# Talking-heads attention and SoLU block: ten source rows in one transfer, pairs in column halves, 64x64 score tiles, and a planner with measured durations

## The chip, the cores and the metric

The kernel runs on one core of a Trainium2 chip. The metric is the device time of one execution in microseconds. An execution has five engines with instruction streams of their own, which run in the order in which they were written and wait for each other by semaphores: TensorE (PE), VectorE (DVE), ScalarE (ACT), GpSimd (POOL), and SyncE (SP), which only issues transfers here. The transfers themselves are made by 16 DMA engines.

## The reference

```python
# q, k, v: (4, 12, 448, 64) = batch, heads, positions, head size
scores = scale * np.matmul(q, k.transpose(0, 1, 3, 2))
scores = np.einsum('bhij,hg->bgij', scores, w_pre)      # mix the heads
scores = scores - np.max(scores, axis=-1, keepdims=True)
attn = np.exp(scores)
attn = attn / (np.sum(attn, axis=-1, keepdims=True) + 1e-09)
attn = np.einsum('bhij,hg->bgij', attn, w_post)         # mix them again
out = np.matmul(attn, v)
# then x = out as (1792, 768)
h = x @ w_in                                            # (768, 1024)
e = np.exp(h - max(h)); sm = e / (sum(e) + 1e-09)
solu = h * sm
ln = (solu - mean(solu)) / np.sqrt(var(solu) + 1e-06) * g_ln
return ln @ w_out                                       # (1024, 768)
```

## The kernel before

For the scores, the first mixing and the second part, numbers of 32 bits are split into a high and a low part of 16 bits, and a product is made of three matmuls (high by low, low by high, high by high). The second mixing and the value products take 32 bits as they are.

A batch has 448 query rows. They are cut into four blocks, of 120 rows or of 88 (`ROWS`, `SIZES`), and a block into units of ten rows (`UN`), 12 units or 9, so that a batch has 45 units and the kernel 180. A unit holds ten query rows for all 12 heads, that is 120 partitions of 448 keys.

- **Scores.** `qk` makes the scores of two heads for a whole block: six matmuls, each 64 rows of the array by the block's 120 or 88 columns, the two heads beside each other in the two row halves. `score_hi` (ACT) and `score_lo` (DVE) write them as high and low parts into the tile `s`, which has a query row on each partition and 12 heads, two parts and 448 keys behind it.
- **Fetch.** The mixing over heads needs the 12 heads on partitions. `fetch` turns each unit by transfers from SBUF to SBUF: five source rows (five partitions of `s`) become 60 partitions of the tile `sr`, one per row and head. A unit takes two such transfers, for its two halves, which lie side by side in `sr`; the two units of a pair lie on partitions 0 to 59 and 64 to 123. All are issued by SP, at line 524. `sr` has four buffers (`AHEAD`), one for each pair, and is free again when the units' row maxima have been taken, since these write their unused full-size output over it.
- **Premix.** `premix` (line 540) mixes the heads for both units of a pair, in twelve matmuls in 64x64 tiles: PSUM tile `pm`, three banks (`m`).
- **Softmax.** `rowmax` (DVE, line 552), `expo` (ACT, line 565, with the sum of the exponentials), `guard` (DVE, line 579, adds 1e-9), `invert` (DVE, line 582), and `weigh` (POOL, line 586), which multiplies the second mixing matrix by the inverse sums into `wr`. There is one of each for every unit.
- **Postmix and values.** `postmix` (line 594) multiplies the exponentials by `wr`; `post_out` (ACT) copies the result into the ring `p_t`; once a block is complete, `av` (line 634) multiplies it by the values, in two bursts of 24 matmuls; `x_hi` and `x_lo` split the result and `x_store` (line 676) writes it out.

Beside this run the loads and the splitting of the next batch's q, k and v; 18 transposing transfers for q and k (`turn_in`, line 427, issued by SP too); and in the last batch the loads and the conversion of `w_in`. After the attention comes the second part, with 14 tiles of 128 tokens.

The order of the whole attention part is written out by a planner, the class `Plan`. Each step is a task with engines and costs, tasks that it follows (`after`), a due time, and the ring of buffers that it holds until other tasks are done. `order` simulates the engines, always places the task that can start earliest, and among those that can start within 0.005 us of it the one due first. A transfer's cost in it is the issue time on SP and a constant latency (`lat`):

```python
                add(
                    ("f",) + g,
                    one(fetch, *g),
                    {"sp": 1.3},
                    after=[("sl", b, blk, h) for h in range(H)],
                    ...
                    until=[("mx",) + p for p in pair],
                    lat=2.7,
                )
```

The tasks' names: `qk`, `sh` and `sl` for the scores, `f` for the fetch, `m` for the premix, `mx`, `ex`, `gd`, `iv`, `w` for the softmax, `o` and `po` for the postmix and its copy, `av`, `xh`, `xl`, `xd` for what follows, `t` for the transposing transfers.

Of the kernel before, what the change touches and what calls it, by code (L numbers as in the profile page):

```python
# [8 lines left out]
F32 = mybir.dt.float32  # L9
# [9 lines left out]
class Plan:  # L19
# [4 lines left out]
    WAIT = 0.2  # L24
    SWITCH = {("m", "o"): 0.087, ("av", "o"): 0.073, ("m", "av"): 0.057, ("o", "qk"): 0.04, ("o", "m"): 0.026}
# [5 lines left out]
    def add(self, key, run, on, after=(), behind=(), due=0.0, ring=None, until=(), lat=0.0, more=()):  # L31

        slots = [list(until)] + [list(x) for x in more]
        self.tasks[key] = (run, on, list(after), due, ring, slots, lat, list(behind))

    def order(self):
        tasks, done, out = self.tasks, {}, []
        held = {r: [] for r in self.size}
        free = {e: 0.0 for _, on, *_ in tasks.values() for e in on}
# [5 lines left out]
        avail = {k for k, n in need.items() if not n}  # L45

        def ready(k, e):
            _, _, after, _, ring, slots, _, _ = tasks[k]
            r = 0.0
            for a in after:  # L50
                end, eng, lat = done[a]
                r = max(r, end + lat + (0.06 if eng == e else self.WAIT))
            for i in range(len(slots) if ring else 0):
                j = len(held[ring]) + i - self.size[ring]
                for a in held[ring][j] if j >= 0 else ():
                    if a not in done:
                        return None
                    r = max(r, done[a][0] + done[a][2] + self.WAIT)
            return r

        last = {}
        while len(out) < len(tasks):
            best = None
            for e, t0 in free.items():
                able = []
                for k in avail:
                    on = tasks[k][1]
                    if e in on:
                        r = ready(k, e)
                        if r is not None:  # L70
                            able.append((max(r, t0), tasks[k][3], k))
                while able:
                    t = min(x[0] for x in able)
                    x = min(
                        (x for x in able if x[0] <= t + 0.005),
                        key=lambda x: (x[1] + 40 * self.SWITCH.get((last.get(e), x[2][0]), 0), str(x[2])),
                    )
                    on = tasks[x[2]][1]
                    if any(max(ready(x[2], f), free[f]) + c < t + on[e] for f, c in on.items() if f != e):
                        able.remove(x)  # L80
                        continue
                    if best is None or (t, x[1]) < best[:2]:
                        best = (t, x[1], e, x[2])
                    break
            t, _, e, k = best
            run, on, _, _, ring, slots, lat, _ = tasks[k]
            free[e] = t + on[e] + 0 * self.SWITCH.get((last.get(e), k[0]), 0)
            last[e] = k[0]
            done[k] = (t + on[e], e, lat)
# [12 lines left out]
def kernel(  # L102
# [30 lines left out]
    WEIGH = {"pool": 0.36}  # L133
    AMV = {"act": 0.95}
# [131 lines left out]
    def chain(key, steps, due, after=()):  # L266

        for i, (eng, f) in enumerate(steps):
# [3 lines left out]
                {eng: 0.3 if eng == "pe" else 0.15},  # L272
# [10 lines left out]
    mk = const.tile([128, 2, UH], F32, name="mk")  # L283
    mh = const.tile([128, UH], F32, name="mh")
# [8 lines left out]
    def mix_load(e):  # L293
        nc.gpsimd.memset(rep, 0.0)
        for i, w in ((0, w_pre), (1, w_post)):
            for lo in (0, 64):
                nc.gpsimd.dma_start(out=rep[lo : lo + HK, i], in_=w.unsqueeze(0).to_broadcast([UH, H, H]))

    def mix_masks(e):
        nc.gpsimd.memset(mk, 1.0)  # L300
        for step, base in ((1, 0), (-1, H - 1)):
            nc.gpsimd.affine_select(
                out=mk,
                in_=mk,
                pattern=[[-64 * step, 2], [-H * step, UH]],
                compare_op=ALU.is_ge,
                fill=0.0,
                base=base,
                channel_multiplier=step,
            )  # L310
        nc.gpsimd.tensor_tensor(out=mh, in0=mk[:, 0], in1=mk[:, 1], op=ALU.add)
# [156 lines left out]
    def qk(b, c, h):  # L468
# [6 lines left out]
        for a, (x, y) in enumerate(((0, 1), (1, 0), (0, 0))):  # L475
            for e in range(2):
                rows = slice(64 * e, 64 * e + 64)
                nc.tensor.matmul(  # L478
                    sps[b, c, h + e],
                    q2[b, g][rows, 2 * j + x, i0 : i0 + n],  # L480
                    k1[b, g][rows, 2 * j + y],
                    start=(a == 0),
                    stop=(a == 2),
                )
# [30 lines left out]

    def fetch(b, u):
        c, r, step, _ = unit_rows(b, u)
        u0, _ = pair_of(b, u)
        if u == u0:
            sr[b, u] = sr_p.tile([128, 2, 2, S], F16, tag="sr", name=f"sr_{b}_{u}")  # L520
        lo = 64 * (u - u0)
        for i in range(2):
            r0 = r + i * UH * step
            nc.sync.dma_start(  # L524
                out=sr[b, u0][lo : lo + HK, i], in_=s_t[b, c][r0 : r0 + (UH - 1) * step + 1 : step]
            )

    def premix(b, u):
# [4 lines left out]
        x = sr[b, u]  # L533
        for j in range(n):
            pmx[b, u + j] = ps_m.tile([UK, 512], F32, tag="m", name=f"pm_{b}_{u + j}")
        for a, (w, z) in enumerate(((wp_hi, 0), (wp_hi, 1), (wp_lo, 0))):
            for j in range(n):
                rows = slice(64 * j, 64 * j + HK)
                for i in range(2):
                    nc.tensor.matmul(  # L540
                        pmx[b, u + j][64 * i : 64 * i + 64, 0:S],
                        w[rows],
                        x[rows, i, z],
# [4 lines left out]
    def rowmax(b, u):  # L548
        nb = nbs[b, u] = st_p.tile([UK, 1], F32, tag="nb", name=f"nb_{b}_{u}")
        u0, _ = pair_of(b, u)  # L550
# [11 lines left out]
    def expo(b, u):  # L562
        sm = sums[b, u] = st_p.tile([UK, 1], F32, tag="sm", name=f"sm_{b}_{u}")
# [10 lines left out]
    def guard(b, u, eng):  # L574
        sm = sums[b, u]
        if eng == "pool":
            nc.gpsimd.tensor_scalar(out=sm, in0=sm, scalar1=1e-9, scalar2=1.0, op0=ALU.add, op1=ALU.mult)
        else:
            nc.vector.tensor_scalar(out=sm, in0=sm, scalar1=1e-9, scalar2=None, op0=ALU.add)

    def invert(b, u):
        nc.vector.reciprocal(out=sums[b, u], in_=sums[b, u])  # L582

    def weigh(b, u, eng):
        w = wr[b, u] = st_p.tile([UK, H * UN], F32, tag="wr", bufs=NWR, name=f"wr_{b}_{u}")
        ENG[eng].tensor_scalar(  # L586
            out=w, in0=wq[0:UK, 0 : H * UN], scalar1=sums.pop((b, u)), scalar2=1.0, op0=ALU.mult, op1=ALU.mult
# [18 lines left out]
    def post_out(b, u, eng):  # L606
        i, n = ring_of(b, u), unit_rows(b, u)[3]
        y = pos.pop((b, u))[:, 0:480].rearrange("p (c i) -> p c i", i=UN)
        copy(eng, p_t[:, :, i : i + n], y[:, :, UN - n : UN])
# [17 lines left out]
    def av(b, blk, g):  # L627
        n = block_rows(b, blk)[1]
        xps[b, blk, g] = ps_x.tile([128, XG, 512 // XG], F32, tag="x", name=f"px_{b}_{blk}_{g}")
        for i in range(XG):  # L630
# [175 lines left out]
    def add_tasks():  # L806
# [5 lines left out]
        add("mixl", mix_load, {"pool": 4.2}, due=0.0, lat=7.5)  # L812
        add("mixm", mix_masks, {"pool": 1.2}, due=1.0)
# [17 lines left out]
        for b in range(B):  # L831
# [3 lines left out]
            for n in "kq":  # L835
                pieces = NP if z else NPAIR
                parts = [(f, n, b, p) for p in range(NPAIR) for f in ("hi", "lo")]
                for i in range(pieces):
# [3 lines left out]
                        {"pool": 1.06} if b else {"sp": 0.65},  # L842
# [5 lines left out]
                        lat=2.6 if b else 4.0 + 0.7 * i + 5.0 * (n == "q"),  # L848
# [4 lines left out]
                for i in range(NP):  # L853
# [3 lines left out]
                        {"dve": 0.93},  # L857
# [8 lines left out]
                for p in range(NPAIR):  # L866
# [4 lines left out]
                        {"pool": 0.8} if b else {"act": 0.61},  # L871
                        after=ready + ([("hi", n, b, p - 1)] if p else before),
# [559 lines left out]
```

## Time and profile before

| | |
|---|---|
| time, median of 3 runs | 804.56 us (802.21 to 805.5) |
| the profiled execution | 801.89 us, of it 800.2 us span |
| PE busy | 684.1 us, 85% of the span |
| DVE busy | 503.2 us, 63% |
| ACT busy | 454.1 us, 57% |
| POOL busy | 264.2 us, 33% |
| mean granted TensorE clock | 0.935 |

The span runs from the first instruction to the last. Busy times are of one profiled execution, and matmuls are pipelined, so that a busy PE is not one at its peak. SP's own instructions, which issue the transfers, are not counted as busy. The clock is a share of full speed, 2.4 GHz; it has two levels, 1.0 and 0.5. The kernel has roughly three stages: the start up to 40 us, the attention up to 550 us, and the second part to the end.

### The profile page before, as it was taken

The numbers are of one execution on the slowest core, as the hardware profiler recorded it, in microseconds if no ns is written. First come the engines' busy times: TensorE is split into PE (matmuls) and PEld (weight loads), VectorE is DVE, ScalarE is ACT, GpSimd is POOL, SyncE is SP. The second block draws the span as 40 slices with busy tenths as digits, with TensorE's granted clock in tenths as the row PEclk, the third lists the DMA queues.
The fourth block names the chain that finished last, engine by engine and source line by source line (L and its number), as shares of the span: only waits on it lengthen the run. The fifth ranks groups of instructions, "written<-read, shape, count | busy, mean of one in ns | idle before, by whom it ended". The sixth has DMA issues, their size and how long they took to land.

```text
span 800.2 us, 16611 instructions
## 1 busy us (share of the span) xinstructions
PE 684.1 (85%) x5986; PEld 443.2 (55%) x5986; DVE 503.2 (63%) x1519; ACT 454.1 (57%) x962; POOL 264.2 (33%) x408
## 2 busy tenths in 40 slices
PE   4878895998987798779699597979998776999998
PEld 3435563765755566557376474757443333556664
DVE  6947883678795578777376798865888866220000
ACT  3746675776676687568477576745455555331111
POOL 5224671124580122563011234232365552330000
PEclk9879998999999799799699799979999997999999
DMA  8044487236458434648614564632646630434111
GB/s 207 13 130 140 143 152 155 106 117 197 158 141 143 124 107 136 189 138 151 145 67 144 177 199 145 166 111 94 178 106 129 134 67 1 90 55 106 57 43 59
DMA packets 114057, 98.45 MB, mean 123 GB/s; under 512 B 69636, under 2 KB 104632, under 8 KB 113976
## 3 DMA queue, kind: packets, MB, share of 16 engines
q1 hardware_dynamic: 108120, 83.62, 40.4%
q0 software_dynamic: 4448, 12.40, 5.6%
q10 hardware_dynamic: 1408, 1.38, 0.7%
q8 instruction: 47, 0.77, 0.4%
q14 instruction: 34, 0.28, 0.1%
HBM read 33.24 MB, written 9.63 MB: 54 GB/s over the span
## 4 chain that ended last, share of the span: by engine, by line
PE 41%; DMA 21%; DVE 15%; SPq 9%; issue 5%; ACT 5%; POOL 4%; DVEq 0%; ACTq 0%; POOLq 0%
PE y L1341 13%; DMA sr<-s 12%; PE po L594 9%; PE px L634 7%; SPq L524 7%; PE ps L478 4%; PE pm L540 4%; DMA cv_wo<-in_moe_w_out_dram 3%; DMA raw_k<-in_k_dram 3%; PE ps_h L797 3%; DVE sr L552 2%; DVE s L495 2%; DMA xl<-xsl 2%; SPq L427 1%; ACT e L565 1%
## 5 line engine op out<-in xcount | busy, mean ns | idle before, releaser
L594 PE MATMUL po<-wr,e 128*112 128x120 f32 x1440 | 196.0, 286 | 14.8 <-POOL wr L586 14.3
L594 PEld LDWEIGHTS po<-wr,e 128*112 128x112 f32 x1440 | 169.0, 187 | 64.7 <-POOL wr L586 32.1
L586 POOL TENSOR_SCALAR wr<-wq,sm 128x120 f32<-128x120 f32 x180 | 72.1, 402 | 335.6 <-DVE sm L582 196.9
L565 ACT ACTIVATE e<-pm,nb,c_exp 128x448 f32<-128x448 f32 x180 | 131.2, 730 | 46.5 <-DVE sr L552 33.2
L552 DVE TENSOR_SCALAR_CACHE_REDUCE sr<-pm,c_nexp 128x448 f32<-128x448 f32 x180 | 118.8, 675 | 54.8 <-PE pm L540 54.1
L230 ACT COPY p_t<-po 112x480 f32<-112x480 f32 x180 | 104.3, 581 | 54.7 <-PE po L594 53.9
L495 DVE SCALAR_TENSOR_TENSOR s<-ps,s 120x448 f16<-120x448 f32 (+1 forms) x192 | 114.5, 616 | 31.1 <-ACT s L490 29.6
L490 ACT ACTIVATE s<-ps 120x448 f16<-120x448 f32 (+1 forms) x192 | 99.5, 544 | 52.1 <-PE ps L478 37.7
L540 PE MATMUL pm<-sr,wp_hi 60*64 60x448 f16 x720 | 78.5, 384 | 49.0 <-DMA sr<-s 35.6
L478 PE MATMUL ps<-k,q 64*120 64x448 f16 (+1 forms) x576 | 84.9, 388 | 10.8 <-DVE s L495 9.9
L797 PE MATMUL ps_h<-wi,xf 128*128 128x512 f16 x396 | 87.9, 379 | 6.7 <-DVE u L1284 6.7
L634 PE MATMUL px<-p_t,raw_v 112*64 112x120 f32 (+1 forms) x1536 | 83.8, 267 | 2.0 <-DVE xsl L226 1.6
L634 PEld LDWEIGHTS px<-p_t,raw_v 112*64 112x64 f32 x1536 | 77.0, 141 | 9.5 <-ACT p_t L230 4.2
L1341 PE MATMUL y<-wo_h,lth 128*128 128x384 f16 (+2 forms) x224 | 72.7, 331 | 9.8 <-ACT wo_h L221 9.8
L1341 PE MATMUL y<-wo_l,lth 128*128 128x384 f16 (+2 forms) x224 | 73.0, 333 | 2.5 <-DVE wo_l L226 2.0
L1341 PE MATMUL y<-wo_h,ltl 128*128 128x384 f16 (+2 forms) x224 | 72.9, 332 | 0.0
L1341 PEld LDWEIGHTS <-lth 128*128 128x128 f16 x448 | 44.3, 99 | 43.8 <-issue 15.4
L797 PEld LDWEIGHTS <-xf 128*128 128x128 f16 x396 | 38.4, 98 | 52.5 <-issue 8.6
L540 PEld LDWEIGHTS <-wp_hi 60*64 60x64 f16 x720 | 19.6, 106 | 83.1 <-issue 45.6
L1349 ACT ACTIVATE o<-y,c_out 128x384 f32<-128x384 f32 (+2 forms) x28 | 16.1, 577 | 70.7 <-PE y L1341 70.7
L478 PEld LDWEIGHTS <-q 64*120 64x120 f16 (+1 forms) x576 | 33.5, 133 | 40.5 <-issue 30.2
L226 DVE SCALAR_TENSOR_TENSOR xsl<-px,x_sc,xsh 128x120 f16<-128x120 f32 (+1 forms) x104 | 27.0, 317 | 28.0 <-ACT xsh L221 21.6
(175 smaller groups left out, 845.4 us busy)
## 6 DMA issues: line engine op xcount, KB each, us to landing
sr<-s SPq DMA_DIRECT2D x360, 105.0 KB
cv_wi<-in_moe_w_in_dram SPq DMA_DIRECT2D x24, 256.0 KB
cv_wo<-in_moe_w_out_dram SPq DMA_DIRECT2D x8, 768.0 KB
raw_k<-in_k_dram POOLq DMA_DIRECT2D x18, 224.0 KB, 6.3
raw_q<-in_q_dram POOLq DMA_DIRECT2D x18, 224.0 KB, 6.0
raw_v<-in_v_dram POOLq DMA_DIRECT2D x18, 224.0 KB, 6.2
xh<-xsh SPq DMA_DIRECT2D x9, 224.0 KB
xl<-xsl SPq DMA_DIRECT2D x9, 224.0 KB
```

The source lines that it names most:

```text
L230: nc.scalar.copy(out=out, in_=in_)
L478: nc.tensor.matmul(sps[b, c, h + e], q2[b, g][rows, 2 * j + x, i0 : i0 + n], k1[b, g][rows, 2 * j + y], start=(a == 0), stop=(a == 2),)
L490: nc.scalar.activation(out=s_t[b, c][0 : y.shape[0], h, 0], in_=y, func=AF.Copy, scale=2.0**-E_S)
L495: nc.vector.scalar_tensor_tensor(out=t[:, h, 1], in0=y, scalar=2.0**-E_S, in1=t[:, h, 0], op0=ALU.mult, op1=ALU.subtract)
L540: nc.tensor.matmul(pmx[b, u + j][64 * i : 64 * i + 64, 0:S], w[rows], x[rows, i, z], start=(a == 0), stop=(a == 2),)
L552: nc.vector.tensor_scalar(out=old, in0=pmx[b, u][:, 0:S], scalar1=c_nexp[0:UK, b : b + 1], scalar2=None, op0=ALU.mult, op1=ALU.min, accum_ ...
L565: nc.scalar.activation(out=ee[b, u], in_=pmx.pop((b, u))[:, 0:S], func=AF.Exp, bias=nbs.pop((b, u)), scale=c_exp[0:UK, b : b + 1], accum_o ...
L586: ENG[eng].tensor_scalar(out=w, in0=wq[0:UK, 0 : H * UN], scalar1=sums.pop((b, u)), scalar2=1.0, op0=ALU.mult, op1=ALU.mult)
L594: nc.tensor.matmul(ps[:, c * 120 : (c + 1) * 120], e[:, c * CP : (c + 1) * CP], w, start=True, stop=True)
L634: nc.tensor.matmul(xps[b, blk, g][e * 64 : e * 64 + 64, i, 0:n], raws["v", b][:, h, c * D : (c + 1) * D], block_view(b, blk, c * H + h), s ...
L797: nc.tensor.matmul(ps[:, n], xx[:, kc, o : o + 128], ww[:, kc, n * 512 : (n + 1) * 512], start=(kc == 0 and a == 0), stop=(kc == KDM - 1 a ...
L1341: nc.tensor.matmul(y, xx[:, kc], ww[:, kc, cut], start=(kc == 0 and a == 0), stop=(kc == KFF - 1 and a == 2),)
```

## The change

`fetch` issues one transfer for each unit of a pair: all ten source rows, onto the partitions 4 to 123 of `sr`. The two units of a pair now lie in the two column halves of the tile, and the two halves of a unit's rows below each other. A premix output so holds one half of the rows of both units, and `post_out` writes it to the ring with an access pattern of two runs. A block's odd last unit still takes two transfers of five rows. The four tiles of `sr` are allocated once, and their first four partitions set to zero by DVE at the start. `rowmax` writes its unused output to a tile `dead` of its own, so that `sr` is free after the premix. `guard` and `invert` are done once for a pair, after both exponentials. `qk` makes the scores of a 120-row block in twelve matmuls of 64x64 tiles (56 columns in half of them). `av` is a task for each of six pairs of heads, of 8 matmuls, in place of two tasks of 24.

The planner's model is another one: each task has an occupancy and a time to its result; hearing of a result costs a time by engine; PE pays 0.093 us when the tile shape changes; a transfer is put on 16 modelled rings with a latency, a size and a rate; the task due first is taken among those that can start within 0.25 us, at 12 units of due time for each microsecond of delay. The scores' due times change, and many costs.

```diff
-    sr_p = st.enter_context(tc.tile_pool(name="sr", bufs=AHEAD))
+    sr_p = st.enter_context(tc.tile_pool(name="sr", bufs=1))
+    dead = sr_p.tile([128, S], F16, name="dead")
...
-                nc.tensor.matmul(
-                    sps[b, c, h + e],
-                    q2[b, g][rows, 2 * j + x, i0 : i0 + n],
+                for lo, hi in ((0, 64), (64, n)) if n > 96 else ((0, n),):
+                    nc.tensor.matmul(
+                        sps[b, c, h + e][lo:hi],
+                        q2[b, g][rows, 2 * j + x, i0 + lo : i0 + hi],
...
+    sr_t = [sr_p.tile([128, 2, 2, S], F16, tag=f"sr{i}", name=f"sr{i}") for i in range(AHEAD)]
+
+    def sr_clear(e):
+        for x in sr_t:
+            nc.vector.memset(x[0:4].rearrange("p z h s -> p (z h s)").bitcast(F32), 0.0)
...
-        lo = 64 * (u - u0)
-        for i in range(2):
-            r0 = r + i * UH * step
-            nc.sync.dma_start(
-                out=sr[b, u0][lo : lo + HK, i], in_=s_t[b, c][r0 : r0 + (UH - 1) * step + 1 : step]
-            )
+        y = s_t[b, c]
+        if n == 2:
+            nc.sync.dma_start(out=sr[b, u0][4:124, u - u0], in_=y[r : r + (UN - 1) * step + 1 : step])
+        else:
+            for e in range(2):
+                r0 = r + e * UH * step
+                nc.sync.dma_start(out=sr[b, u0][4:64, e], in_=y[r0 : r0 + (UH - 1) * step + 1 : step])
...
-        old = sr[b, u0][:, u - u0].rearrange("p z s -> p (z s)").bitcast(F32)
         nc.vector.tensor_scalar(
-            out=old,
+            out=dead,
...
-    def guard(b, u, eng):
-        sm = sums[b, u]
+    def guard(b, u, n):
+        sm = sums[b, u][:, 0:n]
...
-    def invert(b, u):
-        nc.vector.reciprocal(out=sums[b, u], in_=sums[b, u])
+    def invert(b, u, n):
+        sm = sums[b, u][:, 0:n]
+        nc.vector.reciprocal(out=sm, in_=sm)
...
+        g = u - u0
+        x = p_t[:, :, i + UH * g : i + UH * (g + 1)]
+        (pp, np), (cs, cn), (es, en) = x.ap
+        x = bass.AP(x.tensor, x.offset, [[pp, np], [cs, cn], [(ring_of(b, u0 + 1) - i) * es, 2], [es, en]])
+        copy(eng, x, y.rearrange("p c (e i) -> p c e i", e=2))
...
-                    due = at(b, u0 - 6) - STEP * 0.6 * (H - h)
+                    due = at(b, u0 - 4) - STEP * (H - h)
...
-                    {"sp": 1.3},
-                    after=[("sl", b, blk, h) for h in range(H)],
+                    {"sp": 0.77 if n == 2 else 1.54},
+                    after=[("sl", b, blk, h) for h in range(H)] + ["zero"],
...
-                    until=[("mx",) + p for p in pair],
-                    lat=2.7,
+                    until=[("m",) + g],
+                    dma=(10 if n == 2 else 5, 215, 22.7),
...
-                add(("gd",) + g, with_eng(guard, *g), {"dve": 0.1}, after=[("ex",) + g], due=d + 2)
-                add(("iv",) + g, one(invert, *g), {"dve": 0.12}, after=[("gd",) + g], due=d + 2.2)
+                if u == u0:
+                    add(("gd",) + g, one(guard, *g, n), {"dve": (0.06, 0.15)}, after=[("ex",) + p for p in pair], due=d + 2)
+                    add(("iv",) + g, one(invert, *g, n), {"dve": (0.08, 0.166)}, after=[("gd",) + g], due=d + 2.2)
...
+                for p in range(NPAIR):
+                    add(
+                        ("av", b, blk, p),
+                        one(av, b, blk, p),
+                        {"pe": 0.05 + 0.0068 * n},
+                        shape="half",
...
                     ("t", n, b, p),
                     one(turn_in, n, b, p, m),
-                        {"sp": 1.75},
+                        {"sp": 1.57},
...
-                        lat=2.4,
+                        dma=(16, 459, 16.4),
```

And the planner's new parts:

```diff
+    HEAR = {"pe": 0.053, "dve": 0.034, "act": 0.037, "pool": 0.083, "sp": 0.05, "-": 0.0}
+    TURN = 0.093
+    RUSH = 12.0
+    LOOK = 0.25
...
-                        (x for x in able if x[0] <= t + 0.005),
-                        key=lambda x: (x[1] + 40 * self.SWITCH.get((last.get(e), x[2][0]), 0), str(x[2])),
+                        (x for x in able if x[0] <= t + self.LOOK),
+                        key=lambda x: (x[1] + self.RUSH * (x[0] - t), str(x[2])),
...
+                ways, kb, rate = dma
+                end = 0.0
+                for i in range(ways):
+                    rings[i] = max(rings[i], t + (2.6 if e == "pool" else 2.2)) + kb / ways / rate
+                    end = max(end, rings[i])
+                done[k] = (end + 0.2, "dma")
```

## Rows read from the trace of the kernel before

**Rows 1.** Window of the attention: length, busy PE, PEld, DVE, ACT, POOL, clock, DMA, GB/s

```profile
40.00:550.00 510.00, 431.61 (x4500) 305.19 (x4500) 366.59 (x1183) 340.03 (x782) 176.92 (x316) 0.92 0.52 141
```

**Rows 2.** Windows over the eleven stretches of the attention in which PE thins out

```profile
130.00:140.00 10.00, 2.41 (x11) 0.94 (x10) 0.83 (x5) 2.62 (x8) 0.73 (x2) 0.67 0.68 150
...
250.00:264.00 14.00, 5.84 (x56) 4.12 (x58) 4.56 (x17) 5.32 (x14) 0.73 (x2) 0.85 0.89 153
...
380.00:394.00 14.00, 6.19 (x48) 3.62 (x50) 4.26 (x23) 5.72 (x16) 1.46 (x4) 0.71 0.83 156
...
sum 111.00, PE 64.73 PEld 41.61 DVE 61.48 ACT 54.63 POOL 37.75; mean PE 5.88 PEld 3.78 DVE 5.59 ACT 4.97 POOL 3.43
```

**Rows 3.** Windows over the eleven stretches of the attention at the lower clock

```profile
133.30:143.60 10.30, 5.12 (x23) 2.08 (x23) 1.60 (x5) 0.88 (x2) 0.00 (x0) 0.50 0.47 133
...
sum 85.40, PE 64.26 PEld 40.38 DVE 41.24 ACT 37.41 POOL 18.87; mean PE 5.84 PEld 3.67 DVE 3.75 ACT 3.40 POOL 1.72
```

**Rows 4.** Waits of PE from 40 to 550 us: total, times, longest

```profile
PE pm L540 <- DMA sr<-s: 35.6, 34, 6.2
PE po L594 <- POOL wr L586: 14.3, 19, 2.6
PE pm L540 <- ACT e L565: 12.4, 5, 8.1
```

**Rows 5.** Timeline of SP around 130 us: start, length, instructions

```profile
123.33 2.74 SPq L427 DMA_TRANSPOSE k<-hl_k  x1
...
131.03 2.34 SPq L427 DMA_TRANSPOSE q<-hl_q  x1
133.48 9.45 SPq L524 DMA_DIRECT2D sr<-s  x11
```

**Rows 6.** Chain that ended last, 100 to 145 us: start, length, what

```profile
135.42 0.74 SPq L524
...
136.21 3.85 DMA sr<-s
...
140.11 1.28 PE pm L540 x9
```

**Rows 7.** Transfers from 135 to 140 us: queue share, and issues

```profile
q1 hardware_dynamic: 523, 0.54, 34.3%
...
sr<-s SPq DMA_DIRECT2D x7, 105.0 KB
```

**Rows 8.** Instructions of lines 524 and 370: duration min/median/max in ns

```profile
L524 SPq DMA_DIRECT2D sr<-s x360: 720/737/2566, 38.7 to 539.1; - x180
...
L370 SPq DMA_DIRECT2D raw_k<-in_k_dram x2: 386/422/459, 0.8 to 1.2; - x2
```

**Rows 9.** Groups by line: busy, mean ns, idle before

```profile
L565 ACT ACTIVATE e<-pm,nb,c_exp 128x448 f32<-128x448 f32 x180 | 131.2, 730 | 46.5 <-DVE sr L552 33.2 <-DVE sm L582 8.8 <-DVE amx_k L214 1.2
...
L582 DVE RECIPROCAL sm<-sm 128x1 f32<-128x1 f32 x180 | 27.8, 157 | 2.1
...
L579 DVE TENSOR_SCALAR sm<-sm 128x1 f32<-128x1 f32 x180 | 25.9, 146 | 23.1 <-ACT e L565 22.0
```

**Rows 10.** Windows of 10 us with DVE over 92% busy, first and last of twelve

```profile
70.00:80.00 10.00, 8.66 (x117) 6.20 (x119) 9.34 (x33) 5.86 (x15) 5.28 (x10) 1.00 0.51 159
...
540.00:550.00 10.00, 9.84 (x109) 7.10 (x108) 9.31 (x23) 7.04 (x16) 4.39 (x6) 1.00 0.12 30
```

**Rows 11.** Chain near 93 us, a score group and a premix of a pair

```profile
92.61 0.71 PE ps L478 x5
93.32 0.71 PE pm L540 x12
```

**Rows 12.** Timeline of PE near 120 us, postmix bursts

```profile
120.13 2.88 PE L594 MATMUL po<-wr,e 128*112 128x120 f32 x24
...
124.33 1.07 PE L594 MATMUL po<-wr,e 128*112 128x120 f32 x8
```

**Rows 13.** Waits of SP: total, times, longest

```profile
SPq L524 <- DVE s L495: 54.0, 14, 25.9
```

More of the change, by code (lines that the diff above doesn't have):

```diff
@@ L29, in __init__, with add @@
         self.tasks = {}
-    def add(self, key, run, on, after=(), behind=(), due=0.0, ring=None, until=(), lat=0.0, more=()):
+    def add(self, key, run, on, after=(), behind=(), due=0.0, ring=None, until=(), more=(), dma=None, shape="full"):
         slots = [list(until)] + [list(x) for x in more]
-        self.tasks[key] = (run, on, list(after), due, ring, slots, lat, list(behind))
+        tail = {"pe": 0.165, "pool": 0.03}
+        on = {e: x if isinstance(x, tuple) else (x, x + tail.get(e, 0.1)) for e, x in on.items()}
+        self.tasks[key] = (run, on, list(after), due, ring, slots, dma, list(behind), shape)
     def order(self):
@@ L45, in order, with heard @@
         avail = {k for k, n in need.items() if not n}
+        shape, rings = [None], [0.0] * 16
+        def heard(a, e):
+            t, f = done[a]
+            return t + self.FAR.get((f, e), self.HEAR[e])
         def ready(k, e):
-            _, _, after, _, ring, slots, _, _ = tasks[k]
+            _, _, after, _, ring, slots = tasks[k][:6]
             r = 0.0
             for a in after:
-                end, eng, lat = done[a]
-                r = max(r, end + lat + (0.06 if eng == e else self.WAIT))
+                r = max(r, heard(a, e))
             for i in range(len(slots) if ring else 0):
@@ L57, in ready, with turn @@
                         return None
-                    r = max(r, done[a][0] + done[a][2] + self.WAIT)
+                    r = max(r, heard(a, e))
             return r
-        last = {}
+        def turn(k):
+            return self.TURN if shape[0] not in (None, tasks[k][8]) else 0.0
         while len(out) < len(tasks):
@@ L82, in order @@
                     if best is None or (t, x[1]) < best[:2]:
-                        best = (t, x[1], e, x[2])
+                        best = (t, x[1], e, x[2], x[0])
                     break
[L85 to L89, printed above, removed]
+            _, _, e, k, t = best
+            run, on, _, _, ring, slots, dma = tasks[k][:7]
+            if e == "pe":
+                shape[0] = tasks[k][8]
+            free[e] = t + on[e][0]
+            if dma is None:
+                done[k] = (t + on[e][1], e)
+            else:
[5 more added lines that the diff above has]
+                done[k] = (end + 0.2, "dma")
             if ring:
@@ L905, in add_tasks @@
                         due=due,
-                        lat=2.4,
+                        dma=(16, 459, 16.4),
                     )
-            add(("es", b), one(exp_scales, b), {"dve": 0.15}, after=es, due=at(b - 1, 35) if b else T0 - -2)
+            add(("es", b), one(exp_scales, b), {"dve": 0.28}, after=es, due=at(b - 1, 35) if b else T0 - -2)
             for i in range(NPAIR):
@@ L947, in add_tasks @@
                             one(qk, b, c, h),
-                            {"pe": 0.7},
-                            after=before + [("t", n, b, h // 2 if z else h // 2 // GP * GP) for n in "kq"],
+                            {"pe": 0.57},
+                            shape="quarter" if ROWS[b][c] > 96 else "rows",
+                            after=[("t", n, b, h // 2 if z else h // 2 // GP * GP) for n in "kq"],
+                            behind=before,
                             due=due,
@@ L964, in add_tasks @@
                     )
-                    add(("sl", b, c, h), one(score_lo, b, c, h), {"dve": 0.54}, after=[("sh", b, c, h)], due=due + 0.8)
+                    add(("sl", b, c, h), one(score_lo, b, c, h), {"dve": (0.53, 0.62)}, after=[("sh", b, c, h)], due=due + 0.8)
             for u in range(NU):
@@ L989, in add_tasks @@
                     one(premix, *g),
-                    {"pe": 0.72 if u == u0 else 0.0},
-                    after=[("f",) + p for p in pair] + [last] + behind("m") if u == u0 else [("m", b, u0)],
+                    {"pe": 0.57} if u == u0 else {"-": (0.0, 0.0)},
+                    shape="quarter",
+                    after=[("f",) + p for p in pair] + [last] if u == u0 else [],
+                    behind=behind("m") if u == u0 else [("m", b, u0)],
                     due=d if u == u0 else -1000.0,
```

209 lines of the change are left out of this document (110 added, 99 removed).

## The prediction

> **What bounds the kernel now.** I read the windows by stage first. The change touches the attention alone, from 40 to 550 us, and there PE is busy 431.6 of 510 us, DVE 366.6 and ACT 340.0 [rows 1]. PE sets the pace, and 78.4 us of it are idle. Windows of ten microseconds then show that this idle time isn't spread evenly. Eleven stretches, 111 us together, hold 64.73 us of PE work, so 46.3 of the 78.4 idle us lie in them [rows 2]. Elsewhere PE is busy some 92% of the time.
>
> The stretches cost twice. After each longer gap the granted clock falls to 0.50, which is 1.2 GHz: it was at that level for 85.4 us of the attention, and PE worked 64.3 us of these [rows 3]. At full clock that work would have taken about half, so up to 32 us more hang on the gaps. (Not every lower stretch follows from such a gap, and the part of a matmul's record that isn't streaming doesn't halve; 32 is an upper estimate.)
>
> What ends the gaps: the waits of PE name the premix waiting for the fetch, 35.6 us in 34 waits, far ahead of the postmix waiting for its weights (14.3) and of the premix waiting for a bank (12.4) [rows 4]. One gap, looked at closely: from 123 to 133 us SP issues four transposing transfers, each of which holds its queue for 2.3 to 2.7 us, and only then eleven fetches in a row [rows 5]. The last of the fetches that the next premix needs is issued from 135.42 to 136.16 and lands 3.85 us later; then PE goes on [rows 6]. So the path of a gap is the queue of SP, then the issue of fetches one by one, then their transfer.
>
> **The fetch: issue.** It takes 0.737 us of SP, 360 times, 265 us in all [rows 8]. With ten rows in one transfer 176 units take one and the four odd ones two: 184 issues, 136 us, 130 us less on SP. Is a transfer of twice as many rows issued in the same time? No row shows one. A load of three heads by 112 partitions, which has more pieces, took SP 0.42 us [rows 8], so pieces don't set the price; I take 0.74. The upper end is 1.47, two issues, which leaves no gain here.
>
> **The fetch: transfer.** From 135 to 140 us seven fetches were issued, and little else moved. The queue's packets took 34.3% of 16 engines' time and brought 0.54 MB [rows 7]. Five engines are 31%. So a fetch of five source rows uses about five engines, and the next ones, issued behind it, the same ones: with others free the share would have risen. At 0.105 MB each, five came through in 5 us, 1.0 us apiece, longer than the issue. A transfer of ten rows that uses ten engines takes about the same 1.0 us for the whole unit.
>
> The Trainium skill's page "DMA: Bandwidth & Descriptors", section "Why a DMA increments its semaphore by 16 and not by 1", says that the number of engines is the largest, up to 16, that divides the slowest dimension of both sides, and that the lowest-numbered are used: five for 5 rows onto 60 partitions, and ten for 10 onto 120. The 34.3% agrees with five. [...]
>
> A pair needed four issues and the landing, 4 x 0.74 + 3.85 = 6.8 us. It will need two issues, and the landing with one transfer less in the queue, 2 x 0.74 + (3.85 - 1.0) = 4.3 us. That is 2.5 us earlier for the first pair after a gap, and the pairs behind it can come every 2 us rather than every 4. In eleven stretches I take 11 x 2.5 = 27 us of the 46.3. Bounds: nothing, if something else comes last there, and all 46.3, if the pairs that arrive earlier also fill the stock of four before the next gap.
>
> **The clock.** If 27 of 46.3 us of gaps go, I let the same share of the 32 us go: 19 us, between 0 and 32.
>
> **DVE.** `guard` and `invert` run 92 times instead of 180: 88 x (0.146 + 0.157) = 27 us less [rows 9]. DVE is the last engine only in the stretches with conversions; of the 51 windows of ten microseconds in the attention it is over 92% busy in twelve [rows 10]. 27 x 12/51 = 6 us, between 0 and 27.
>
> **What I cost at nothing.**
> - The merged `guard` and `invert` hold the first unit's weights until the second's exponential is done, 0.73 us later [rows 9]. PE has scores, value products or the unit before to do meanwhile. Without that cover it is 88 x 0.73 = 64 us; this is the rival below.
> - The scores in twelve 64x64 matmuls instead of six: a premix of twelve such matmuls took 0.71 us, five of the six of a score group just before it 0.71 too [rows 11]. Scores and premix now have one tile shape.
> - The value products in six bursts instead of two: a postmix of 24 matmuls took 2.88 us, 0.96 for each 8, a burst of 8 alone 1.07 [rows 12]. So a break costs about 0.11 us; 16 blocks x 4 more bursts is 7 us at most. A score group beside a premix saves such a break, 72 x 0.11 = 8 us at most. They cancel; both ends go into the range.
> - The four memsets at the start run while DVE waits for the first load. `dead` in place of `sr` leaves the row maximum as it is and frees the buffer a row maximum earlier. `post_out` moves as many elements.
> - The planner. It reorders everything, and no row prices an order. What can be said: before, it took 1.3 us of SP and 2.7 us of latency for a unit's fetch, while a pair needed 6.8; a model with rings is nearer to what the rows show. I add nothing for it.
>
> **Sum.** 27 + 19 + 6 = 52 us. The profiled execution took 801.9 us (span 800.2, and 1.7 around it): 750. The median of the runs lies 2.7 us above that execution, so 753 us.
>
> **Rivals.**
> - *The gaps go altogether.* The buffers fill, and the order keeps SP ahead: 46.3 + 32 + 6 = 84 us, 721 us. For it: elsewhere PE already works at 92%. Against: DVE and ACT are at 72% and 67% of the attention, and in-order queues with loads and transposes stay.
> - *The transposing transfers stay in front.* Three stretches, 23.6 us idle, lie behind them (130, 250 and 380 us) [rows 2, 5]. If these keep, the others give 22.8 x 27/46.3 = 13, the clock 9, DVE 6: 777 us. For it: they aren't changed, and their 2.3 us is more than the 1.57 that the planner counts.
> - *The ten rows move at the rate of five engines.* Only two issues a pair are saved: 11 x 1.48 = 16 us, the clock 11, DVE 6: 772 us. Against it: the 34.3% [rows 7]. [...]
> - *The scores become last.* SP waited 54.0 us, 14 times, for a block's last score piece [rows 13]. The last pair of heads is now due 1.6 steps of 2.25 us later, 3.6 us. If the order follows that, the fetch starts 1.1 us later than it gained, up to 12 us in eleven stretches, against DVE's 6: 799 to 811, and about 804 us, no change, in the middle.
> - *Slower: the merged denominators.* PE already waits 19 times for the weights [rows 4]. If every pair's first postmix comes 0.73 us late, 64 us are lost, with 7 for the split value products: 753 + 71 = 824 us. It decides from about 52 of these 71 us, so when seven pairs in ten show the delay. Against it: the units are several ahead of the postmix in the order, four exponentials are buffered, and the two postmixes then run as one burst.
>
> **How the numbers follow.** Chances: the forecast 0.46 (its own range 738 to 770), gaps gone 0.15, transposes in front 0.14, same engines 0.06, scores last 0.07, slower 0.12. A change within 0.5% (4 us) can't be told from none. So faster 0.81, the same 0.07, slower 0.12. The range leaves out the slower case and about half of the best one: 722 to 803 us.
>
> **What would show it.** In the changed kernel: 184 issues of `fetch` near 0.74 us each; a DMA share of about 0.6 while only fetches run; PE's wait for the fetch well under 35.6 us, some 15; idle time of PE in the attention near 50 us; a mean clock there about 0.95; DVE 27 us less. The forecast is wrong if PE's wait for `wr` grows beyond 40 us, if the fetches' issue costs 1.4 us, or if the gaps lie where they lay, behind the transposes or the loads.

## The result and the profile after

The changed kernel takes 728.68 us (median of 4 runs, 725.9 to 729.22), the kernel before on the same chip 803.9. The ratio is 0.906, with an interval from 0.903 to 0.909. The forecast was 753 us with a range from 722 to 803. So direction and range hold, but the gain is 75 us where 52 were worked out, and it lies near the rival in which the gaps go altogether. One execution of the first run with extra load, 1214.76 us, and one of the run with everything but the fetch, 858.29 us, were slow ones, and the ratios and rows below leave them out.

First the windows of the changed kernel, with the columns of [rows 1]. It ends at 477 us, just behind the last premix, as 550 us did before; the second line is the rest.

```profile
40.00:477.00 437.00, 397.61 (x4983) 292.65 (x4984) 366.21 (x1011) 345.04 (x788) 179.90 (x323) 0.98 0.59 165
477.00:727.50 250.50, 224.89 (x1279) 120.05 (x1276) 106.76 (x251) 90.06 (x139) 75.58 (x53) 0.98 0.38 88
```

The attention takes 437 us instead of 510, and the second part its 250 us as before, so that the whole of the 72.7 us of span lies in the attention. PE's idle time there falls from 78.4 to 437 - 397.6 = 39.4 us, by 39 us; its busy time falls from 431.6 to 397.6, 34 us, while the mean clock rises from 0.92 to 0.98.

The waits of PE in the attention, with the columns of [rows 4]:

```profile
PE po L625 <- POOL wr L617: 19.4, 27, 1.7
PE ps L502 <- DVE s L519: 7.1, 15, 2.1
PE pm L570 <- DMA sr<-s: 6.0, 4, 2.3
```

The wait for the fetch is down from 35.6 to 6.0 us, and the longest from 6.2 to 2.3. The wait for the weights is a little longer than before and now the first. The chain that ended last names other work too. Its line by engine in the kernel before, and then in the changed one:

```profile
PE 41%; DMA 21%; DVE 15%; SPq 9%; issue 5%; ACT 5%; POOL 4%; DVEq 0%; ACTq 0%; POOLq 0%
```

```profile
PE 46%; DVE 30%; DMA 8%; ACT 6%; POOL 5%; issue 3%; SPq 1%; ACTq 0%; POOLq 0%; DVEq 0%
```

Transfers and SP's queue made up 30% of the chain and make up 9%. DVE took their place, at twice its share.

Now the fetch itself, the instructions of its two lines in the changed kernel:

```profile
L553 SPq DMA_DIRECT2D sr<-s x176: 768/773/3046, 42.9 to 452.8; - x176
L557 SPq DMA_DIRECT2D sr<-s x8: 793/1610/1747, 54.6 to 456.7; - x8
```

The issue of ten rows costs 0.773 us, against 0.737 for five. For the transfer I take a stretch in which nothing but ten-row fetches is issued, one behind the other, 126 to 130 us: the row of the queue there, and behind it the same from 424.5 to 427.5 us of the kernel before, with five-row fetches only (packets, MB, share of 16 engines' time).

```profile
q1 hardware_dynamic: 597, 1.00, 65.6%
```

```profile
q1 hardware_dynamic: 227, 0.37, 32.4%
```

32.4% of 16 is about five engines, 65.6% about ten. Five rows are 60 pieces of 1,792 bytes, 0.1075 MB. They took 0.1075/0.37 x 3 = 0.87 us on five engines, and ten rows 0.215/1.00 x 4 = 0.86 us on ten: twice the engines brought twice the rate.

Loads that the change doesn't touch got faster as well, those of k and v by some 2 us and those of q hardly. The loads issued by POOL, before and after (the last number is the median of us from issue to landing):

```profile
raw_k<-in_k_dram POOLq DMA_DIRECT2D x18, 224.0 KB, 6.3
raw_q<-in_q_dram POOLq DMA_DIRECT2D x18, 224.0 KB, 6.0
raw_v<-in_v_dram POOLq DMA_DIRECT2D x18, 224.0 KB, 6.2
```

```profile
raw_k<-in_k_dram POOLq DMA_DIRECT2D x18, 224.0 KB, 4.0
raw_q<-in_q_dram POOLq DMA_DIRECT2D x18, 224.0 KB, 5.6
raw_v<-in_v_dram POOLq DMA_DIRECT2D x18, 224.0 KB, 4.5
```

That pointed to something that all transfers share, and led to a theory that the prediction doesn't have, here called load: the five engines that carried every fetch had about as much to do as the attention's time allowed. An estimate from the trace: the fetches' packets (1,792 bytes each) took 1810 us in all, 362 on each of the five. The whole share of 0.52 in [rows 1] is 0.52 x 16 x 510 = 4243 engine-us, and less the fetches that leaves 152 us for each of the 16 engines, if it is spread evenly. That is 514 us for each of the five in an attention of 510 us. In the changed kernel the same packets took 1916 us, 192 on each of ten engines, and the rest (0.59 x 16 x 437 less 1916) is 138 us on each of the 16: 330 us in 437. No packet at all was under way in 5% of the attention's time before, and in 19% after.

So the five were short of time, but not at every moment. From 410 to 420 us of the kernel before, nearly nothing moved (a share of 0.04), and PE was busy throughout:

```profile
410.00:420.00 10.00, 10.00 (x105) 7.34 (x105) 7.92 (x27) 8.81 (x21) 1.46 (x4) 1.00 0.04 14
```

The prediction's own theory is called latency: at the head of each gap a pair's issues and its transfer take too long. A third is called order: the planner, with its new model, places fetches and scores better.

### The profile page after: what moved, and what is told of

The parts are those of the page before. It is cut to its first block, busy times and chain, and to the rows that moved or that the text cites. A ratio compares the mean times of both kernels' runs of the same rounds, so it can differ in the third digit from the quotient of the medians.

```text
span 727.5 us, 17255 instructions
## 1 busy us (share of the span) xinstructions
PE 642.6 (88%) x6418; PEld 427.1 (59%) x6418; DVE 506.5 (70%) x1345; ACT 454.8 (63%) x960; POOL 271.1 (37%) x418
## 4 chain that ended last, share of the span: by engine, by line
PE 46%; DVE 30%; DMA 8%; ACT 6%; POOL 5%; issue 3%; SPq 1%; ACTq 0%; POOLq 0%; DVEq 0%
PE y L1397 14%; PE po L625 13%; PE px L675 6%; DVE dead L580 5%; PE pm L570 5%; PE ps L502 5%; DVE s L519 4%; DMA sr<-s 4%; PE ps_h L838 3%; POOL wo L776 2%; DVE cv_wo L773 2%; ACT e L596 2%; DVE hl_q L247 2%; DMA raw_q<-in_q_dram 2%; DVE cv_wo L768 1%
## 5 line engine op out<-in xcount | busy, mean ns | idle before, releaser
L625 PE MATMUL po<-wr,e 128*112 128x120 f32 x1440 | 179.3, 278 | 19.6 <-POOL wr L617 19.4
L625 PEld LDWEIGHTS po<-wr,e 128*112 128x112 f32 x1440 | 160.0, 182 | 48.2 <-POOL wr L617 34.7
L580 DVE TENSOR_SCALAR_CACHE_REDUCE dead<-pm,c_nexp 128x448 f16<-128x448 f32 x180 | 121.8, 677 | 24.4 <-PE pm L570 16.0
L251 ACT COPY p_t<-po 112x480 f32<-112x480 f32 x180 | 109.9, 626 | 16.8 <-PE po L625 16.1
L675 PE MATMUL px<-p_t,raw_v 112*64 112x120 f32 (+1 forms) x1536 | 90.0, 264 | 5.6 <-ACT p_t L251 2.3
L502 PE MATMUL ps<-k,q 64*64 64x448 f16 (+2 forms) x1008 | 82.7, 362 | 11.5 <-DVE s L519 7.1
L1397 PE MATMUL y<-wo_h,lth 128*128 128x384 f16 (+2 forms) x224 | 72.7, 331 | 9.8 <-ACT wo_h L242 9.8
L570 PE MATMUL pm<-sr,wp_hi 64*64 64x448 f16 (+1 forms) x720 | 58.0, 367 | 9.3 <-DMA sr<-s 6.0
L502 PEld LDWEIGHTS <-q 64*64 64x64 f16 (+2 forms) x1008 | 33.8, 108 | 40.9 <-issue 21.0
L596 ACT ACTIVATION_READ_ACCUMULATOR e<-pm,nb,c_exp 128x1 f32 x180 | 38.4, 213 | 0.0
L570 PE MATMUL pm<-sr,wp_lo 64*64 64x448 f16 (+1 forms) x360 | 36.5, 355 | 0.0
```

The lines of the kernel that those rows point to most:

```text
L251: nc.scalar.copy(out=out, in_=in_)
L502: nc.tensor.matmul(sps[b, c, h + e][lo:hi], q2[b, g][rows, 2 * j + x, i0 + lo : i0 + hi], k1[b, g][rows, 2 * j + y], start=(a == 0), stop= ...
L570: nc.tensor.matmul(pmx[b, u + i][64 * e : 64 * e + 64, 0:S], w[rows], sr[b, u][rows, e, z], start=(a == 0), stop=(a == 2),)
L580: nc.vector.tensor_scalar(out=dead, in0=pmx[b, u][:, 0:S], scalar1=c_nexp[0:UK, b : b + 1], scalar2=None, op0=ALU.mult, op1=ALU.min, accum ...
L596: nc.scalar.activation(out=ee[b, u], in_=pmx.pop((b, u))[:, 0:S], func=AF.Exp, bias=nbs.pop((b, u)), scale=c_exp[0:UK, b : b + 1], accum_o ...
L625: nc.tensor.matmul(ps[:, c * 120 : (c + 1) * 120], e[:, c * CP : (c + 1) * CP], w, start=True, stop=True)
```

## The experiments

Ratios are to the kernel before, measured beside each run; it took 800.5 to 801.8 us there.

### The fetch alone, with the old planner

The kernel before with the parts of the change that the new fetch needs. The order of the instructions on PE is that of before, one by one.

```diff
-        for i in range(2):
-            r0 = r + i * UH * step
-            nc.sync.dma_start(
-                out=sr[b, u0][lo : lo + HK, i], in_=s_t[b, c][r0 : r0 + (UH - 1) * step + 1 : step]
-            )
+        if n == 2:
+            nc.sync.dma_start(out=sr[b, u0][4:124, u - u0], in_=y[r : r + (UN - 1) * step + 1 : step])
...
                     {"sp": 1.3},
-                    after=[("sl", b, blk, h) for h in range(H)],
+                    after=[("sl", b, blk, h) for h in range(H)] + ["zero"],
...
                     lat=2.7,
```

> The kernel before, its planner and its costs, with the new fetch alone: ten rows in one transfer, column halves, the zeroed partitions, the separate unused output. The scores' tiles, the denominators, the value bursts and the planner stay as before. Theory fetch (the transfers were what the gaps waited for, whatever the order): about 755 to 765 us, PE's wait for the fetch under 15 us. Theory order (the old planner puts fetches late behind transposes and loads, and faster ones come late as well): 785 to 800 us, with the gaps near 130, 250 and 380 us still there.

731.93 us, ratio 0.914 (0.907 to 0.921). The attention up to the last value product, of the kernel before and then of this one, and this one's wait for the fetch:

```profile
40.00:560.50 520.50, 442.11 (x4639) 313.31 (x4638) 368.45 (x1192) 343.50 (x789) 177.66 (x318) 0.92 0.52 141
40.00:490.00 450.00, 411.88 (x4634) 297.03 (x4634) 373.98 (x1193) 347.84 (x789) 176.61 (x318) 0.98 0.58 163
```

```profile
PE pm L548 <- DMA sr<-s: 4.4, 6, 1.3
```

Nearly all of the gain is there without the new planner, without the merged denominators, the new score tiles and the finer value bursts. The theory of order falls. That of latency, 755 to 765 us, is short by more than 20 us. PE's idle time falls from 78.4 to 38.1 us, by 40, and its busy time by 442.1 - 411.9 = 30 us.

### Everything but the fetch

The changed kernel with two transfers of five rows for each unit, and a planner that knows it.

```diff
-            nc.sync.dma_start(out=sr[b, u0][4:124, u - u0], in_=y[r : r + (UN - 1) * step + 1 : step])
+            for e in range(2):
+                r0 = r + e * UH * step
+                nc.sync.dma_start(
+                    out=sr[b, u0][4 + HK * e : 4 + HK * (e + 1), u - u0],
+                    in_=y[r0 : r0 + (UH - 1) * step + 1 : step],
+                )
...
-                    {"sp": 0.77 if n == 2 else 1.54},
+                    {"sp": 1.54},
-                    dma=(10 if n == 2 else 5, 215, 22.7),
+                    dma=(5, 215, 22.7),
```

> The changed kernel with the fetch of a unit again in two transfers of five rows each (to the new places), and its planner told so (issue 1.54 us, five modelled rings). Theory fetch: most of the gain is lost, 775 to 800 us, PE's wait for the fetch back above 25 us. Theory order: most of the gain stays, 735 to 750 us, since the planner starts the fetches early enough.

809.71 us, ratio 1.009 (1.006 to 1.011): slower than before by a little. Its attention up to the last value product and its waits:

```profile
40.00:570.00 530.00, 442.04 (x5119) 321.29 (x5119) 376.05 (x1032) 353.76 (x795) 169.97 (x310) 0.92 0.51 139
```

```profile
PE po L630 <- POOL wr L622: 35.5, 32, 5.6
PE ps L502 <- DVE s L519: 27.5, 42, 3.3
PE pm L575 <- DMA sr<-s: 6.1, 9, 1.2
```

This run went beyond what either theory expected, and it is the one to remember when reading waits: PE waits for the fetch no longer than in the changed kernel, 6.1 us, and yet the whole takes 81 us more than that one. The time shows in waits for DVE and POOL instead. My reading is that the planner, told of slow transfers, puts other work ahead of each premix; no run shows that by itself. The name at a wait isn't its cause in any case.

### Halves in the changed kernel's own order

The same two transfers, with the planner's costs untouched, so that the order stays.

> The changed kernel in its own order, with each unit's fetch in two transfers of five rows. Nothing else moves, so its time less that of the changed kernel is the price of issue and engines together under that order. By the terms of the prediction (2.5 us for each pair at the head of a gap, about fifteen block changes) and the clock: 40 to 60 us more, 770 to 790 us. If the order has slack everywhere: under 10 us more.

787.95 us, ratio 0.982 (0.977 to 0.986), 59 us more than the changed kernel, as the theory of latency had it in size. Its attention and three waits:

```profile
40.00:547.00 507.00, 424.43 (x5122) 309.38 (x5120) 370.67 (x1026) 351.25 (x797) 180.52 (x326) 0.94 0.51 145
```

```profile
PE ps L502 <- DVE s L519: 21.8, 21, 6.1
PE pm L575 <- DMA sr<-s: 19.4, 17, 3.2
...
PE ps L502 <- DMA k<-hl_k: 5.9, 1, 5.9
```

### Two issues, ten engines

The changed kernel in its own order, a unit's fetch in two transfers of all ten rows, one for the high and one for the low parts.

```diff
+            for z in range(2):
+                nc.sync.dma_start(
+                    out=sr[b, u0][4:124, u - u0, z], in_=y[r : r + (UN - 1) * step + 1 : step, :, z]
+                )
```

> The changed kernel in its own order, with each unit's fetch in two transfers that each read all ten source rows, one for the high and one for the low part: two issues, but ten source rows and so, by the prediction, ten engines for each. If the issue on SP is what counts, it is as slow as the run with halves; if the engines count, it stays within 10 us of the changed kernel. A DMA share of about 0.6 while only fetches run speaks for ten engines.

740.75 us, ratio 0.922 (0.918 to 0.927). Against the last run the bytes, the issues and the order are the same, and the pieces are smaller; that ten engines carry them instead of five is worth 47 of the 59 us, or more if the smaller pieces cost something. The other 12 us are the second issue, or the smaller pieces of this run; which of the two wasn't tried apart.

```profile
40.00:502.00 462.00, 410.65 (x5121) 301.73 (x5120) 370.01 (x1025) 348.99 (x796) 180.16 (x326) 0.97 0.57 159
```

```profile
PE pm L573 <- DMA sr<-s: 7.9, 9, 2.2
```

### Load on the five engines, with nobody waiting for it

So far a fetch on five engines was both slower itself and a load for others. This run parts the two: each unit's own fetch stays on ten engines, and a five-row transfer follows it, to memory that nobody reads.

```diff
             nc.sync.dma_start(out=sr[b, u0][4:124, u - u0], in_=y[r : r + (UN - 1) * step + 1 : step])
+            nc.sync.dma_start(
+                out=scr[len(pads) % 8][:, 0 : 2 * S],
+                in_=y[r : r + (UH - 1) * step + 1 : step].rearrange("r h z s -> r h (z s)"),
+            )
```

> The changed kernel in its own order; behind each unit's fetch SP issues one more transfer of five source rows of the same block, into memory that nobody reads. So there are two issues for each unit, as with two issues on ten engines (740.75 us), but the first five engines carry as much as with the halves (787.95 us), while each unit's own fetch stays one transfer over ten engines and nobody waits for the extra one. Theory latency (a pair's own issues and transfer are too long at the head of a gap): 735 to 745 us. Theory load (the five engines have more to do than they can do in the attention's time, and everything queues behind): 765 to 795 us.

808.58 us, ratio 1.008 (1.005 to 1.011). It was run a second time, and the rows below are of that run.

> The run with extra load on five engines once more, on the same chip as its counterpart on ten: about 808 us. In its profile PE should wait for the fetch and for what the late fetches hold up, and the DMA engines' mean share in the attention should be no higher than with the halves plus the extra bytes, since only five of sixteen are full.

805.43 us, ratio 1.007 (1.004 to 1.009). With two issues this would be about 740.75 us by the theory of latency; the extra load costs 65 us more. It may also hold up the second fetch of a pair, which is issued behind it, by the 0.87 us of a five-row transfer: some 10 us in eleven gaps, an estimate, and far from 65. But both runs lie above the 765 to 795 us of the theory of load too, and 17 us or more above the run with halves, in which the five engines carry as many bytes. What the extra transfers cost beyond that stays open. The attention and its waits:

```profile
40.00:567.00 527.00, 436.71 (x5118) 318.56 (x5115) 368.34 (x1023) 349.12 (x794) 180.18 (x326) 0.91 0.60 176
```

```profile
PE ps L502 <- DVE s L519: 27.2, 19, 8.8
PE pm L578 <- DMA sr<-s: 24.8, 15, 3.1
...
PE ps L502 <- DMA k<-hl_k: 6.8, 1, 6.8
...
PE ps L502 <- DMA q<-hl_q: 4.5, 2, 3.7
```

The loads by POOL are slower again than in the changed kernel, by 0.4 to 1.6 us. This by itself proves little, for in the run with the fetch alone, a fast one, k took 5.8 us.

```profile
raw_k<-in_k_dram POOLq DMA_DIRECT2D x18, 224.0 KB, 5.6
raw_q<-in_q_dram POOLq DMA_DIRECT2D x18, 224.0 KB, 6.0
raw_v<-in_v_dram POOLq DMA_DIRECT2D x18, 224.0 KB, 4.9
```

The mean share of the DMA engines is 0.60, hardly above that of the changed kernel in its shorter time: a mean over 16 engines can't show how full five of them are.

### The same extra bytes on ten engines

```diff
+            nc.sync.dma_start(
+                out=scr[len(pads) % 8][:, 0:S], in_=y[r : r + (UN - 1) * step + 1 : step, :, 0]
+            )
```

> As the run with extra load, with the same bytes in the extra transfer, but read from all ten source rows (the high parts only), so by the prediction spread over ten engines. Theory load on five engines: the first five have three quarters of what they had with the halves, so most of the loss goes, 740 to 765 us. If the extra bytes or their destination in memory did the harm, and not which engines carry them: about 805 us again.

767.81 us, ratio 0.960 (0.956 to 0.963), a little above what was expected. It ran on the same chip as the repetition above, 38 us less for the same bytes, though in smaller pieces. So it matters how many engines carry them. But 27 us above the run with two issues remain: more bytes do harm on ten engines as well. Whether their destination in memory adds to that stays open.

### The kernel before, with half of the bytes

```diff
-                out=sr[b, u0][lo : lo + HK, i], in_=s_t[b, c][r0 : r0 + (UH - 1) * step + 1 : step]
+                out=sr[b, u0][lo : lo + HK, i, 0], in_=s_t[b, c][r0 : r0 + (UH - 1) * step + 1 : step, :, 0]
...
-                        x[rows, i, z],
+                        x[rows, i, 0],
```

> The kernel before, unchanged in order, issues and engines, but each fetch moves the high parts only, half of the bytes; the premix takes the high parts in place of the low ones, so the low parts of the scores are left out of the result. Theory latency: a transfer shorter by half under 0.74 us of issue saves under 2 us for each of the eleven gaps, and the clock with it: 765 to 785 us. Theory load: the five engines have time again, 730 to 750 us, with PE's wait for the fetch under 10 us.

729.61 us, ratio 0.910 (0.906 to 0.914). All instructions of the kernel before, 360 issues on five engines, PE's in their old order, and the time of the changed kernel. Only the bytes of the fetches are halved, and with them nearly the engines' time: a packet takes 41 ns at the median instead of 75. The result leaves out the low parts of the scores. The queue from 340 to 345 us, with fetches alone, takes 18.7% of 16 engines' time, as much as three of the five have. Then the attention and the wait for the fetch:

```profile
q1 hardware_dynamic: 391, 0.32, 18.7%
```

```profile
40.00:486.00 446.00, 413.07 (x4636) 299.18 (x4636) 368.34 (x1192) 340.80 (x790) 176.36 (x318) 0.97 0.44 121
```

```profile
PE pm L540 <- DMA sr<-s: 2.5, 5, 1.0
```

The loads by POOL land as soon as in any other run, or sooner:

```profile
raw_k<-in_k_dram POOLq DMA_DIRECT2D x18, 224.0 KB, 3.8
raw_q<-in_q_dram POOLq DMA_DIRECT2D x18, 224.0 KB, 4.0
raw_v<-in_v_dram POOLq DMA_DIRECT2D x18, 224.0 KB, 3.6
```

### Denominators by unit

The changed kernel with `guard` and `invert` for each unit, the planner told.

```diff
-                if u == u0:
-                    add(("gd",) + g, one(guard, *g, n), {"dve": (0.06, 0.15)}, after=[("ex",) + p for p in pair], due=d + 2)
+                add(("gd",) + g, one(guard, *g), {"dve": (0.06, 0.15)}, after=[("ex",) + g], due=d + 2)
```

> The changed kernel with guard and inverse for each unit again, and its planner told so. By the prediction's term the merge saves 27 us of DVE and 6 us of time: 732 to 738 us. If the merge delays the weights: under 725 us. PE's wait for the weights tells the second from the first.

> The changed kernel as it is, for comparison on the same chip: 724 to 732 us by every theory.

727.68 us, ratio 0.908 (0.905 to 0.911); the changed kernel beside it 728.56, ratio 0.908 (0.905 to 0.911). The merge is worth nothing either way. PE's wait for the weights tells that it does delay them, since by units it is less than half of the 19.4 us above:

```profile
PE po L627 <- POOL wr L619: 8.3, 12, 1.5
```

Nor does it free 27 us of DVE. The two groups in the changed kernel:

```profile
L607 DVE TENSOR_SCALAR sm<-sm 128x2 f32<-128x2 f32 (+1 forms) x92 | 20.1, 219 | 18.1 <-ACT e L596 17.4
...
L611 DVE RECIPROCAL sm<-sm 128x2 f32<-128x2 f32 (+1 forms) x92 | 15.2, 165 | 2.9
```

They sum to 35.3 us, against 53.7 in [rows 9], 18 us less, mostly because the addition for two columns takes 219 ns instead of 146.

## Why the prediction was right, and where it fell short

**What bounds.** Right: the gaps in PE's work hung on the fetch, and each cost twice, as idle time and as clock. The idle time fell by 39 us and PE's busy time by 34. With the fetch alone, where PE runs the same matmuls as before, they fell by 40 and 30 us, both inside the upper ends that I gave, 46.3 and 32.

**Issue.** Right: ten rows are issued in 0.773 us.

**Engines.** Right in number, five and then ten, by the shares of 32.4% and 65.6%, and in that ten rows take no longer than five: 0.86 and 0.87 us, somewhat under the 1.0 that I took from a stretch with other packets in it. The Trainium skill's page "DMA: Bandwidth & Descriptors", section "Why a DMA increments its semaphore by 16 and not by 1", counts the engines so, and the trace agrees. The same page of the Trainium skill, section "Rules for kernel authors", advises one transfer in place of two to disjoint partition halves, because both halves would use all 16 engines. The advice held here and the reason didn't: the halves used five engines. Two issues on five engines took 787.95 us, two on ten 740.75.

**The term for the transfer.** This is the step that failed. I priced it as latency at the heads of eleven gaps, 11 x 2.5 = 27 us, and gave 46.3 us as the bound. Measured were 39 us. The row that I used for the number of engines, one fetch after the other on the same five, also says that these five are busy for up to 1.0 us of each fetch, and 360 times that, with a share of all other transfers, is about the attention's whole time. I multiplied the issues (265 us of SP) and never the engines. The run with two issues on ten engines, 47 us faster than the one with halves, and the old kernel with half of the bytes, 730 us, show that the time on these engines was the cause. The load on five engines without any waiter, 805 us, and the same bytes on ten, 768 us, show that it counts even where nobody waits for the bytes, and that it matters how many engines share it. Two things the runs don't tell apart: the sum over the attention, and the rate of the fetches behind a gap, where a pair's four transfers run one after the other on the same five engines. In each of these runs both changed together.

That the time lies in the range even so is owed to its lower end, 722 us, which reaches nearly to the rival with all gaps gone (721 us). The forecast itself rests on the term that failed.

**The clock.** The mechanism was right and the size followed the gaps: 30 us of PE's busy time with the fetch alone, and not 19. The other 4 us come with the other steps of the change.

**DVE.** Wrong: 6 us were forecast and nothing was measured, 727.68 against 728.56 us.

**The steps costed at nothing** (planner, score tiles, value bursts, the merge's delay). Right as a sum: the fetch alone takes 731.93 us, the changed kernel 728.68 and 728.56, with overlapping intervals. Without the fetch they cost 0.9% together in the planner's order for halves (809.71 us) and gained 1.8% in the changed kernel's own order (787.95 us).

**The rivals.** What happened lies between the forecast of 753 and the rival in which the gaps go altogether, 721 us, and nearer to the rival. From 40 us on, PE is busy for under 7.5 us in only two windows of ten microseconds of the attention (from 60 and from 440 us), where it was in twelve. The transposing transfers didn't stay in front. The last of them start at 330.6 and 332.2 us in the changed kernel, and no gap follows; first the instructions, then the window with the columns of [rows 2]:

```profile
L450 SPq DMA_TRANSPOSE q<-hl_q x9: 1566/3679/5019, 101.4 to 332.2; - x9
L450 SPq DMA_TRANSPOSE k<-hl_k x9: 1427/1574/4162, 112.1 to 330.6; - x9
```

```profile
330.00:340.00 10.00, 9.85 (x140) 7.12 (x132) 6.68 (x21) 10.00 (x25) 1.00 (x4) 1.00 0.87 184
```

The scores didn't become last, and the merged denominators delay the weights without deciding.

## What to carry to other kernels

Add up what each DMA engine carries, not only what each transfer takes and what the mean share over all engines says: here a mean of 0.52 hid five engines with work for nearly all of the attention's time. An access pattern whose outermost dimension is 5 kept a transfer on five engines; twice the rows in one transfer was worth 70 us with PE's order the same. And test a load by putting it back with nobody waiting for it. Waits alone don't tell: PE's wait for the fetch was 6 us both in the changed kernel and in one that took 81 us more.

## What was not expected of the hardware

The extra transfers, which nobody waited for, cost more than the theory of load gave them: 805 us, where the run with halves, with as many bytes on the same five engines, took 788. And loads by another engine felt the fetches: those of k, q and v landed after 6.0 to 6.3 us at the median in the kernel before and after 3.6 to 4.0 with half the bytes in the fetches. That they were held up by the five busy engines is my reading; no run shows it by itself, and in the changed kernel q still took 5.6 us.
